# Banded attention, routing and two feed-forward layers on one core: gate products by two blocks, and idle matmuls in other places

## The chip, the cores and the metric

The program runs on one NeuronCore of a Trainium2 chip. TensorE (PE) multiplies; its weight loads are shown apart as PEld. VectorE (DVE), ScalarE (ACT) and GpSimd (POOL) work on vectors, and SyncE (SP) issues most DMAs. The metric is the device time of one launch in microseconds (us). Shorter is better.

## What is computed

Three stages follow each other: attention with a window of 128 and 4 sink keys, a mixture of 8 experts in which every expert takes exactly 192 of the 1536 tokens, and a dense layer with silu. The reference, cut:

```python
def _attn_ref(q, k, v, n_sink, window):          # q, k, v: (2, 8, 768, 64)
    ...
    keep = is_sink | in_window
    scores = np.where(keep, scores, -1000000000.0)
    ...
    return np.matmul(a, v).astype(np.float32)

def _moe_ref(x, w_gate, w1, w2):                 # x: (1536, 512), w_gate: (512, 8)
    logits = x @ w_gate
    order = np.argsort(-logits.flatten())        # best pair first, 192 tokens for each expert
    ...
        h = np.maximum(x[mask] @ w1[e], 0.0)
        out[mask] = h @ w2[e]

def _moe2_ref(x, w_in, w_out):                   # w_in: (512, 2048)
    h = x @ w_in
    g = h * (1.0 / (1.0 + np.exp(-h)))
    return (g @ w_out).astype(np.float32)
```

The gate's logits are linear in the attention's output. So the kernel multiplies the values with the gate's weights once (a "gate product": 8 extra columns for each head), and the attention's product with the values then yields the logits beside the output.

## The kernel before

**Attention** (`attention_band`) goes over 12 blocks of 128 queries (two batches of six) with 8 heads each. One loop over `n`, one step for each block and head, writes the order of all engines by hand: each engine works through its instructions in the order in which this loop issues them. In step `n` it issues the scores of heads `n` and `n+1` (`s_mm`, even `n`, L255), the exponential of head `n-2` on ACT (L277), the transposition of head `n-5` (`tr`, L291), then row maxima on DVE (L268), and at the end of the step the product of head `n-13` with the values (`pv`, L334 for the block's own keys, L336 for the block before, L339 for the sinks). Three queues (`act_now`, `act_bg`, `dve_now`) hold small pieces of work, of which `feed` takes one at a time between the large ones. Hooks at some `n` unpack weights of the last layer on DVE (L854 to L870).

The gate products stand in `vw`, once for each block `i`, eight steps after the block begins (`VL`): four matmuls (L374) with the transposed values as stationary operand (128 columns, a fresh one for each pair of heads) and 16 gate columns as moving operand, then one copy on ACT (L375) into columns `D:D+E` of `va`, which `pv` reads from step `8i + 13` on. `sinks` takes the first four rows of a batch's first block from there (L380 to L383).

PSUM is shared: the pool's name "s" has four buffers, for scores, for `misc()` (gate products, sinks, `sink_tr`) and for the routing.

**Routing** (`Route`) finds a threshold for each expert. Two shortened rounds run in the last steps of attention, then `run` makes four full rounds (`iterate`). A round is a chain: DVE chooses (L587 to L604), DVE and ACT compare with a grid (L622, L627), PE counts (L635), DVE decides (L644), PE raises the thresholds (L645). `result` then ranks the tokens (L751, L753), makes one-hot rows `R` on DVE (L777) and multiplies them on PE (L778, L781) into `idx`, by which POOL gathers the rows of the first experts (L965).

`warm(k)` issues `k` idle matmuls of 512 columns on PE (L796), whose result nobody reads. `HOLD` says how many stand behind each of the first three full rounds (10), behind the last one (4) and behind the gather (18); `HOT` how many stand between the ranks and the product with `R` (4). PE works strictly in this order, so what stands behind idle matmuls starts after them.

**Experts and dense layer**: `gathered_t` transposes gathered rows (L1002; two more idle matmuls after each of the first two, L1006), then long rows of matmuls follow (L1039, L1042 and others) until the end.

Of the kernel before, what the change touches and what calls it, by code (L numbers as in the profile page):

```python
# [11 lines left out]
F32 = mybir.dt.float32  # L12
# [3 lines left out]
AF = mybir.ActivationFunctionType  # L16
# [5 lines left out]
P = 128  # L22
B, H, S, D = 2, 8, 768, 64
NB = S // P
NT = B * NB
DM = H * D
KW = P + 4
E = 8
# [152 lines left out]

VW = D + E + 1
HH = H // 2
LT, LP, LS, VL = 5, 13, 6, 8
PB = {"s": 4, "tp": 2, "X": 2}
WARM = (8,) + (2,) * 5

# [1 line left out]
def attention_band(tc, qd, kd, va_d, vt_d, vs_d, sel_d, wbd_d, eye_d, n_sink, ident, x_d, L_sb, pp, hooks={}):  # L189
    nc = tc.nc  # L190
    with ExitStack() as ctx:
        cp = ctx.enter_context(tc.tile_pool(name="a_c", bufs=1))
        wp = ctx.enter_context(tc.tile_pool(name="a_w", bufs=2))

        kall = cp.tile([P, NB, HH, KW], F32, name="kall")
        va = cp.tile([P, NB, H, VW], F32, name="va")
        vts, Q = {}, {}

        def load(i, step=HH):
            b, j = divmod(i, NB)  # L200
            Q[i] = wp.tile([P, HH, P], F32, name="qr", bufs=4)
            for p in range(0, HH, step):
                nc.sync.dma_start(kall[:, j, p:p + step], kd[b, j][:, p:p + step])
                nc.sync.dma_start(Q[i][:, p:p + step], qd[b, j][:, p:p + step])

        def load_v(i):
            b, j = divmod(i, NB)
            vts[i] = wp.tile([P, 4, P], F32, name="vt", bufs=3)
            nc.sync.dma_start(vts[i], vt_d[b, j])
            nc.sync.dma_start(va[:, j], va_d[b, j])  # L210

        load(0, 1)
        wbd = cp.tile([P, 4, 2 * E], F32, name="wbd")
        nc.scalar.dma_start(wbd, wbd_d)
        sel = cp.tile([4, 96], F32, name="sel")
        nc.scalar.dma_start(sel, sel_d)
# [23 lines left out]
        nc.gpsimd.affine_select(out=mask[:, 1, 4:4 + n_sink], in_=mask[:, 1, 4:4 + n_sink], pattern=[[-1, n_sink]],  # L240
                                compare_op=OP.is_ge, fill=NEG, base=0, channel_multiplier=1)

        A, TS, AT, X, XS, LW = {}, {}, {}, {}, {}, {}
        ats = [cp.tile([97, P], F32R, name=f"ats{k}") for k in range(2)]
        for t in ats:
            nc.gpsimd.tensor_copy(t[96:97, :], later[0:1, 0:1].to_broadcast([1, P]))
# [1 line left out]
        def s_mm(n):  # L248
            i, h = divmod(n, H)
            j = i % NB  # L250
            b0 = max(j - 1, 0)
            for o in range(2):
                s = pp.tile([P, 512], F32, name="s", bufs=PB["s"])[:, :2 * KW].rearrange("p (a k) -> p a k", a=2)
                d = slice(o * D, (o + 1) * D)
                nc.tensor.matmul(s[:, :j - b0 + 1], Q[i][d, h // 2], kall[d, b0:j + 1, h // 2], start=True, stop=True)  # L255
                TS[n + o] = s
# [29 lines left out]
        def tr(n):  # L286
            i, h = divmod(n, H)
            g, r = divmod(h, 4)
            if r == 0:
                AT[i, g] = pp.tile([P, 4, P], F32, name="tp", bufs=PB["tp"])  # L290
            nc.tensor.transpose(AT[i, g][:, r], A[i][:, h, 4:], ident)  # L291
            if r == 3:
                act_now.append(lambda: tr_out(i, g))
# [9 lines left out]
                                        base=0, channel_multiplier=1)  # L303
            AT[i, g] = f, d

        def misc():
            return pp.tile([P, 512], F32, name="s", bufs=PB["s"])[:, :P]

        zero = cp.tile([P, 512], BF, name="zero")
        nc.vector.memset(zero, 0.0)  # L310
# [3 lines left out]
        def warm(k):  # L314
            for _ in range(k):
                nc.tensor.matmul(idle, zero[:, :P], zero, start=True, stop=True)
# [50 lines left out]
                dve_now.append(lambda: nc.vector.tensor_reduce(L_sb[:, i], lw.rearrange("p h e -> p e h"), AX.X,  # L367
                                                               OP.add))

        def vw(i):  # L370
            j = i % NB
            pf = misc()[:, :H * E]
            for c in range(4):
                nc.tensor.matmul(pf[:, c * 2 * E:(c + 1) * 2 * E], vts[i][:, c], wbd[:, c], start=True, stop=True)  # L374
            act_now.append(lambda: nc.scalar.activation(va[:, j, :, D:D + E], pf.rearrange("p (h e) -> p h e", h=H),  # L375
                                                        AF.Copy))

        def sinks(b):
            m = misc()[:96, :H * E].rearrange("p (h e) -> p h e", h=H)
            nc.tensor.matmul(m, sel, va[0:4, 0, :, D:D + E], start=True, stop=True)  # L380
            dve_now.append(lambda: nc.vector.tensor_tensor(vsf[b][:96, :, D:D + E], m, eye, OP.mult))
            dve_now.append(lambda: nc.vector.tensor_copy(vsr[b], vsf[b]))
            dve_now.append(lambda: nc.vector.tensor_tensor(vsr[b][64:96], vsf[b][64:96],  # L383
                                                           vsr[b][64:96].bitcast(F32), OP.subtract))

        def feed(*qs):
            for q in qs:
                if q:
                    f = q.popleft()
                    if f:  # L390
                        f()
                    return

        act_now, act_bg, dve_now = deque(), deque(), deque()
        warm(WARM[0])
        NH = NT * H
        for n in range(NH + LP + 5):
            i, h = divmod(n, H)
            if n < NH and n % 2 == 0:
                s_mm(n)  # L400
            if n < len(WARM) - 1:
                warm(WARM[n + 1])
            for f in hooks.get(n, ()):
                if f is None:
                    while dve_now:
                        feed(dve_now)
                else:
                    f()
            if 0 <= n - 2 < NH:
                s_exp(n - 2)  # L410
            if 0 <= n - LT < NH:
                tr(n - LT)
            feed(act_now, act_bg)
            if n < NH and n % 2 == 0:
                s_merge(n)
                s_merge(n + 1)
            feed(dve_now)
            if n < NH:
                s_max(n)
            feed(dve_now)  # L420
            feed(act_now, act_bg)
            it, ht = divmod(n - LS, H)
            if ht == H - 1 and 0 <= it < NT:
                sink_tr(it)
            if n < NH and h == 0:
                if i == 1:
                    nc.sync.dma_start(vsf[1][:96], vs_d[:96, 1])
                if i + 2 < NT:
                    load_v(i + 2)
                if i + 3 < NT:  # L430
                    load(i + 3)
            it, ht = divmod(n - VL, H)
            if ht == 0 and 0 < it < NT and it != NB:
                vw(it)
            if n in (VL + 2, NB * H + VL - 5):
                vw(n // (NB * H) * NB)
            if n in (VL + 4, NB * H + VL - 3):
                sinks(n // (NB * H))
            if 0 <= n - LP < NH:
                pv(n - LP)  # L440
        while act_now or act_bg or dve_now:
# [14 lines left out]
)  # L456
NA, RP = 4, 6
HOT, HOLD = 4, (10, 4, 18)


def levels(low, high):
# [24 lines left out]
class Route:  # L486
# [30 lines left out]
    def open(self, wp, psum):  # L517
        self.wp, self.psum = wp, psum
        self.it = 0
        self.work = None  # L520
        self.V = wp.tile([P, NT, E], F32, name="V", bufs=1)

    def scale(self, L, n):
# [122 lines left out]
        ]  # L646
        return steps, [partial(grid_act, t) for t in range(na)] + grids, counts, rise

    def iterate(self, na):
        for part in self.iteration(NT, na):  # L650
            for s in part:
                s()

# [7 lines left out]
    def run(self, L, idx, nit, more, bg=lambda k: None, speculate=lambda: None):  # L661
        self.work = self.psum("s")
        for k in range(nit):
            bg(k)
            self.iterate(NA)
            self.warm(HOLD[k + 1 == nit])
            if k == 0:
                self.scaled()
        bg(nit)
        badi = self.result(idx)  # L670
        speculate()
        self.warm(HOLD[2])
        self.further(badi, L, idx, more, speculate)

    def result(self, idx):
# [113 lines left out]
        nc.vector.scalar_tensor_tensor(idx.rearrange("p m s -> p s m"), im[:, :, 0], float(P), idf, OP.mult, OP.add)  # L789
        return badi  # L790

    def warm(self, k):
        m = self.psum("tp")
        g = self.G[:, :4].rearrange("p t h -> p (t h)")
        for _ in range(k):
            self.nc.tensor.matmul(m, self.onesb, g, start=True, stop=True)  # L796

# [496 lines left out]
def lay_out_band(x):  # L1294
    c = np.ascontiguousarray
    v, wg = x["v"], x["moe_w_gate"]
    va = np.zeros((B, NB, P, H, VW), v.dtype)
    va[..., :D] = v.transpose(0, 2, 1, 3).reshape(B, NB, P, H, D)
    va[..., D + E] = 1.0
    vs = np.zeros((97, B, H, VW), v.dtype)  # L1300
    vr = vs[:96].reshape(3, H, 4, B, H, VW)
    eye = np.zeros((3, H, 4, H, E), np.float32)
    for h in range(H):
        vr[:, h, :, :, h, :D] = v[:, h, :4].transpose(1, 0, 2)
        vr[:2, h, :, :, h, D + E] = 1.0
        eye[:, h, :, h, :] = 1.0
    vs[96, :, :, D + E] = 1.0e-9
    wbd = np.zeros((2, D, 4, 2, E), wg.dtype)
    for o in range(2):
        wbd[o, :, :, o, :] = wg.reshape(4, 2, D, E)[:, o].transpose(1, 0, 2)  # L1310
    return {
        "va": va,
        "vt": c(v.transpose(0, 1, 3, 2).reshape(B, 4, 2 * D, NB, P).transpose(0, 3, 2, 1, 4)),
        "vs": vs,
        "sel": np.tile(np.eye(4, dtype=np.float32), (1, 24)),
        "wbd": wbd.reshape(P, 4, 2 * E),
        "eye": eye.reshape(96, H, E),
    }

# [49 lines left out]
```

## Time and profile before

| | |
|---|---|
| time, three runs | 571.62, 571.73, 574.24 us (median 571.73) |
| the profiled execution | 575.38 us, of which its span is 573.7 us |
| PE busy | 558.0 us (97%) |
| DVE busy | 301.8 us (53%) |
| ACT busy | 259.5 us (45%) |
| POOL busy | 228.2 us (40%) |
| attention in that span | to 110.3 us |
| four full rounds, ranks, gather | 111.7 to 145.4 us |
| experts and dense layer | from 145.4 us on |

A time in the profile is a time from the start of the span. Busy shares are averages over stages with different limits; what binds a stage is read in it alone. The granted clock (PEclk) is a share of TensorE's full 2.4 GHz: 1.00 or 0.50 (1.2 GHz).

### The profile page before, as it was taken

To read this page: it belongs to the slowest core of one execution; us is meant where nothing else is said; L and a number is where in the kernel's file an instruction comes from. 1 tells how busy PE (TensorE), PEld (TensorE's weight loads), DVE (VectorE), ACT (ScalarE), POOL (GpSimd) and SP (SyncE) were. 2 spreads that over 40 slices of the span, in tenths; PEclk is the share of its full clock that TensorE was granted. 3 is DMA by queue.
4 is the path that set the end of the run, shared out by engine and by line. 5 is a ranking of instruction groups with operands and counts; after the bars stand their busy time and mean duration, and the time that the engine had idled before them with its cause. 6 is when DMAs were issued, how large, how long until landed. Compare 5 with 4: busy or idle time off the path is not lost.

```text
span 573.7 us, 9287 instructions
## 1 busy us (share of the span) xinstructions
PE 558.0 (97%) x3398; PEld 492.4 (86%) x3398; DVE 301.8 (53%) x855; ACT 259.5 (45%) x498; POOL 228.2 (40%) x207
## 2 busy tenths in 40 slices
PE   9999999789999999999999999999999999999996
PEld 4778778634899999999999998998899899899884
DVE  3796898973434443443338774665438843141312
ACT  4545454562467776776653452442222332222120
POOL 3434334394599999999993000000000000000224
PEclk9999999986999999999999999999999999999998
DMA  7997562244456666667661340323010000000012
GB/s 223 361 373 253 191 200 92 93 154 125 130 188 231 220 223 219 215 226 231 210 206 37 120 129 9 111 78 107 0 38 1 0 1 0 1 0 2 37 74 110
DMA packets 26367, 74.86 MB, mean 130 GB/s; under 512 B 3338, under 2 KB 4874, under 8 KB 26316
## 3 DMA queue, kind: packets, MB, share of 16 engines
q1 hardware_dynamic: 24128, 67.85, 35.8%
q0 software_dynamic: 1920, 6.29, 3.2%
q8 instruction: 29, 0.48, 0.4%
q14 instruction: 22, 0.18, 0.1%
q10 hardware_dynamic: 268, 0.06, 0.1%
HBM read 67.90 MB, written 6.29 MB: 129 GB/s over the span
## 4 chain that ended last, share of the span: by engine, by line
PE 68%; issue 3%; POOL 3%; ACT 1%; DVE 1%; POOLq 0%; another core or an unknown queue 0%; ACTq 0%
PE mm L1039 8%; PE m L1062 8%; PE h L1118 7%; PE h L1120 7%; PE h L1119 7%; PE acc L1148 7%; PE acc L1149 7%; PE acc L1147 7%; PE mm L1042 4%; PE m L1065 3%; POOL out L1131 2%; PE mm L1062 1%; PE mm L1002 1%; PE mm L1065 1%; POOL wr L895 0%
## 5 line engine op out<-in xcount | busy, mean ns | idle before, releaser
L895 POOL TENSOR_TENSOR wr<-raw,wr 128x1024 fp32r<-128x1024 f32 x64 | 150.9, 2389 | 10.7 <-ACT wr L892 7.1
L1131 POOL DMA_INDIRECT out<-osum,idx x12 | 11.8, 980 | 251.8 <-DVE osum L1155 250.7
L1122 ACT ACTIVATE sg<-h 128x384 f32<-128x384 f32 x64 | 31.4, 491 | 170.2 <-PE h L1120 156.4
L1124 DVE TENSOR_TENSOR gt<-sg,gt 128x384 fp32r<-128x384 f32 x64 | 39.3, 615 | 123.2 <-ACT gt L1123 122.7
L1118 PE MATMUL h<-x,wr 128*128 128x384 f32 x256 | 86.6, 338 | 0.0
L1119 PE MATMUL h<-x,wr 128*128 128x384 f32 x256 | 86.6, 338 | 0.0
L1120 PE MATMUL h<-x,wr 128*128 128x384 f32 x256 | 86.5, 338 | 0.0
L1039 PE MATMUL mm<-xg,wr 128*128 128x384 f32 x256 | 74.8, 362 | 1.6 <-DVE ht L1024 1.1
L1148 PE MATMUL acc<-wr,gt 128*128 128x512 f32 x192 | 76.0, 396 | 0.0
L1149 PE MATMUL acc<-wr,gt 128*128 128x512 f32 x192 | 76.0, 396 | 0.0
L1147 PE MATMUL acc<-wr,gt 128*128 128x512 f32 x192 | 76.0, 396 | 0.0
L892 ACT ACTIVATE wr<-raw 128x1024 fp32r<-128x1024 f32 x64 | 66.7, 1052 | 9.3 <-ACTq L681 6.8
L1062 PE MATMUL m<-ht,wr 128*128 128x384 f32 x224 | 66.1, 362 | 0.0
L1042 PE MATMUL mm<-xg,wr 128*128 128x192 f32 x256 | 64.3, 251 | 0.0
L1065 PE MATMUL m<-ht,wr 128*128 128x192 f32 x224 | 56.3, 252 | 0.0
L277 ACT ACTIVATE A<-t,nm 128x132 f32<-128x132 f32 x96 | 36.4, 400 | 33.7 <-DVE nm L268 33.4
L1039 PEld LDWEIGHTS mm<-xg,wr 128*128 128x128 f32 x256 | 48.1, 188 | 2.5 <-PE mm L1042 1.0
L1119 PEld LDWEIGHTS h<-x,wr 128*128 128x128 f32 x256 | 48.1, 188 | 1.4
L1118 PEld LDWEIGHTS h<-x,wr 128*128 128x128 f32 x256 | 48.1, 188 | 1.3
L1042 PEld LDWEIGHTS mm<-xg,wr 128*128 128x128 f32 x256 | 49.0, 191 | 0.1
L1120 PEld LDWEIGHTS h<-x,wr 128*128 128x128 f32 x256 | 48.1, 188 | 0.0
L1149 PEld LDWEIGHTS acc<-wr,gt 128*128 128x128 f32 x192 | 36.1, 188 | 8.7
(160 smaller groups left out, 1014.5 us busy)
## 6 DMA issues: line engine op xcount, KB each, us to landing
raw<-in_w SPq DMA_DIRECT2D x64, 512.0 KB, 3.6
raw<-in_wi SPq DMA_DIRECT2D x16, 512.0 KB, 3.9
raw<-in_wo SPq DMA_DIRECT2D x16, 512.0 KB, 4.2
va<-in_va SPq DMA_DIRECT2D x12, 292.0 KB, 5.0
vt<-in_vt SPq DMA_DIRECT2D x12, 256.0 KB, 4.7
x_d<-x SPq DMA_DIRECT2D x12, 256.0 KB, 3.2
kall<-in_kd SPq DMA_DIRECT2D x10, 264.0 KB, 5.4
qr<-in_qd SPq DMA_DIRECT2D x10, 256.0 KB, 5.6
```

The lines of the kernel that those rows point to most:

```text
L892: nc.scalar.activation(w[:, 0, sl], src(), AF.Copy)
L895: (nc.vector if k in self.late else nc.gpsimd).tensor_tensor(w[:, 1, sl], src(), w[:, 0, sl].bitcast(F32), OP.subtract)
L1039: nc.tensor.matmul(mm[:, b, :2 * CAP], w[:, 0, fb, d, o:o + P], x[:, d].rearrange("p a t -> p (a t)"), start=d == 0, stop=False, skip_grou ...
L1042: nc.tensor.matmul(mm[:, b, :CAP], w[:, 1, fb, d, o:o + P], x[:, d, 0], start=False, stop=d == 3, skip_group_check=True)
L1062: nc.tensor.matmul(mm[:, d % 2, :2 * CAP], w[:, 0, d // 2, f, o:o + P], ht[:, f].rearrange("p a t -> p (a t)"), start=c == 0 and f == 0, s ...
L1065: nc.tensor.matmul(mm[:, d % 2, :CAP], w[:, 1, d // 2, f, o:o + P], ht[:, f, 0], start=False, stop=last, skip_group_check=True)
L1118: nc.tensor.matmul(hv, w[:, 0, d, o:o + P], x2[:, d, 0, sx], start=d == 0, stop=False)
L1119: nc.tensor.matmul(hv, w[:, 0, d, o:o + P], x2[:, d, 1, sx], start=False, stop=False)
L1120: nc.tensor.matmul(hv, w[:, 1, d, o:o + P], x2[:, d, 0, sx], start=False, stop=d == 3)
L1147: nc.tensor.matmul(a, gt[:, 0, ts], w[:, 0, f], start=f == 0, stop=False)
L1148: nc.tensor.matmul(a, gt[:, 0, ts], w[:, 1, f], start=False, stop=False)
L1149: nc.tensor.matmul(a, gt[:, 1, ts], w[:, 0, f], start=False, stop=f == 3)
```

## The change

Gate products are made for two blocks at a time. The values of two blocks now stand side by side in one tile. The gate's weights are the stationary operand, padded with zeros to 32 columns for each pair of heads; the four pairs of heads write to partitions 0, 32, 64 and 96 of one PSUM tile, so each uses its own group of 32 columns of the PE array. The moving operand is the values, 256 columns. Since this gives the products transposed, ACT copies them to SBUF (`vwt`), two steps of the loop later PE transposes them back (`vw_tr`), and ACT writes one piece for each block to `va`. The table `VWS` says at which step each part stands: blocks 0 and 1 singly (8, 10, 13, 16), the pairs `m` = 1 to 5 at `16m + 5` and `16m + 8`; the sinks at 11 and 58 (12 and 53 before).

In the routing, 12 idle matmuls stand ahead of the first full round's counts, 5 behind each of the first three rounds (10 before), 6 behind the last one (4), 3 between ranks and product (4), and 26 behind the gather (18).

```diff
-LT, LP, LS, VL = 5, 13, 6, 8
+LT, LP, LS = 5, 13, 6
+VWS = {8: [((0, (0,)), 0)], 10: [((0, (0,)), 1)], 11: [((0,), 2)], 13: [((0, (1,)), 0)], 16: [((0, (1,)), 1)],
+       58: [((1,), 2)]}
+for m in range(1, NT // 2):
+    VWS[2 * H * m + 5], VWS[2 * H * m + 8] = [((m,), 0)], [((m,), 1)]
...
         def load_v(i):
             b, j = divmod(i, NB)
-            vts[i] = wp.tile([P, 4, P], F32, name="vt", bufs=3)
-            nc.sync.dma_start(vts[i], vt_d[b, j])
+            if i % 2 == 0:
+                vts[i // 2] = wp.tile([P, 4, 2, P], F32, name="vt", bufs=2)
+            nc.sync.dma_start(vts[i // 2][:, :, i % 2], vt_d[b, j])
             nc.sync.dma_start(va[:, j], va_d[b, j])
...
-        def vw(i):
-            j = i % NB
-            pf = misc()[:, :H * E]
+        def vw(m, os=(0, 1)):
+            k = len(os)
+            pf = misc(k * P)
             for c in range(4):
-                nc.tensor.matmul(pf[:, c * 2 * E:(c + 1) * 2 * E], vts[i][:, c], wbd[:, c], start=True, stop=True)
-            act_now.append(lambda: nc.scalar.activation(va[:, j, :, D:D + E], pf.rearrange("p (h e) -> p h e", h=H),
-                                                        AF.Copy))
+                nc.tensor.matmul(pf[c * 4 * E:(c + 1) * 4 * E], wbd[:, c],
+                                 vts[m][:, c, os[0]:os[-1] + 1].rearrange("p o t -> p (o t)"),
+                                 start=True, stop=True, skip_group_check=True)
+            f = VT[m, os] = wp.tile([P, 2 * P], F32, name="vwt", bufs=1)
+            act_now.append(lambda: nc.scalar.activation(f[:, :k * P], pf, AF.Copy))
+
+        def vw_tr(m, os=(0, 1)):
+            k = len(os)
+            pt = misc(k * P).rearrange("p (o z) -> p o z", o=k)
+            f = VT.pop((m, os))
+            for q in range(k):
+                nc.tensor.transpose(pt[:, q], f[:, q * P:(q + 1) * P], ident)
+
+            def put(q, o):
+                nc.scalar.activation(
+                    va[:, (2 * m + o) % NB, :, D:D + E].rearrange("p (c k) e -> p c k e", k=2),
+                    pt[:, q].rearrange("p (c k e) -> p c k e", c=4, e=E)[:, :, :2], AF.Copy)
+            act_now.extend(partial(put, q, o) for q, o in enumerate(os))
...
-            it, ht = divmod(n - VL, H)
-            if ht == 0 and 0 < it < NT and it != NB:
-                vw(it)
-            if n in (VL + 2, NB * H + VL - 5):
-                vw(n // (NB * H) * NB)
-            if n in (VL + 4, NB * H + VL - 3):
-                sinks(n // (NB * H))
+            for at, f in VWS.get(n, ()):
+                (vw, vw_tr, sinks)[f](*at)
...
-HOT, HOLD = 4, (10, 4, 18)
+HOT, HOLD = 3, (12, 5, 6, 26)
...
-    def iterate(self, na):
-        for part in self.iteration(NT, na):
+    def iterate(self, na, warm=0):
+        g = self.G
+        parts = self.iteration(NT, na)
+        self.warm(warm if g is not None else 0, g)
+        for part in parts:
...
-            self.iterate(NA)
-            self.warm(HOLD[k + 1 == nit])
+            self.iterate(NA, HOLD[0] if k == 0 else 0)
+            self.warm(HOLD[1 + (k + 1 == nit)])
...
-        self.warm(HOLD[2])
+        self.warm(HOLD[3])
```

The first place is PE at a block in the middle of attention, eight steps after an even block began (X is the product with the values, tp a transposition, s the shared PSUM name). Before:

```order
L255 MATMUL s<-kall,qr 128x264 x2
L291 MATMUL tp<-ident,A 128x128
L374 MATMUL s<-wbd,vt 128x16 x4
L334 MATMUL X<-va,atd 128x73
L336 MATMUL X<-va,at 128x73
L339 MATMUL X<-vsr_144,ats_158 128x292
```

In the changed kernel the same stretch of PE, from step `16m + 5` to `16m + 8`:

```order
L325 MATMUL s<-ident,a_1183 96x128
L379 MATMUL s<-vt,wbd 32x256 x4
L339 MATMUL X<-va,atd 128x73
L341 MATMUL X<-va,at 128x73
L260 MATMUL s<-kall,qr 128x264 x2
L296 MATMUL tp<-ident,A 128x128
L339 MATMUL X<-va,atd 128x73
L341 MATMUL X<-va,at 128x73
```

The four matmuls of 16 columns, once a block, became four of 256 columns and 32 rows of output, once in two blocks. They stand right behind the sinks' transposition, and one product with the values (L339, L341) parts them from the next scores (L260). Two transpositions follow three steps later, where L374 stood.

The second place is ACT over the same steps (A the exponentials, at the evacuated transposition). Before:

```order
L277 ACTIVATE A<-t,nm 128x132 x4
L297 ACTIVATE at<-tp 128x512
L277 ACTIVATE A<-t,nm 128x132
L375 ACTIVATE va<-s 128x8x8
L277 ACTIVATE A<-t,nm 128x132 x3
```

In the changed kernel:

```order
L302 ACTIVATE at<-tp 128x512
L282 ACTIVATE A<-t,nm 128x132 x2
L383 ACTIVATE vwt<-s 128x256
L282 ACTIVATE A<-t,nm 128x132 x2
L302 ACTIVATE at<-tp 128x512
L282 ACTIVATE A<-t,nm 128x132
L393 ACTIVATE va<-s 128x8x8 x2
```

Two copies for two blocks became one of 256 columns and two small ones; the large one stands behind two exponentials and an evacuation.

The third place is PE where the first full round begins (G the grid, r_dlt the thresholds' steps). Before, the counts follow the last raising at once:

```order
L635 LDWEIGHTS G
L635 MATMUL s<-oh,G 128x8
L645 LDWEIGHTS r_dlt
L645 MATMUL s<-sel,r_dlt 128x8
L635 LDWEIGHTS G
L635 MATMUL s<-oh,G 128x8
```

In the changed kernel the idle matmuls stand between, of which one is shown and 12 are issued; the counts (L650) follow them:

```order
L650 LDWEIGHTS G
L650 MATMUL s<-oh,G 128x8
L660 LDWEIGHTS r_dlt
L660 MATMUL s<-sel,r_dlt 128x8
L816 LDWEIGHTS r_ones
L816 MATMUL tp<-G,r_ones 128x512
```

The counts of the first full round moved behind 12 matmuls that wait for nothing.

## Rows read from the trace of the kernel before

**Rows 1.** Windows by stage: length, then busy us of each engine, clock, DMA.

```profile
core 0: us, PE busy (x) PEld busy (x) DVE busy (x) ACT busy (x) POOL busy (x), PEclk, DMA share, GB/s
20.00:52.00 32.00, 32.00 (x253) 25.93 (x251) 26.34 (x137) 15.19 (x42) 12.68 (x27) 1.00 0.90 326
60.00:76.00 16.00, 16.00 (x112) 12.22 (x110) 15.69 (x73) 8.21 (x21) 5.98 (x12) 1.00 0.56 189
100.00:110.00 10.00, 10.00 (x98) 9.51 (x97) 9.59 (x50) 5.19 (x14) 4.59 (x9) 1.00 0.33 107
112.95:119.75 6.80, 4.68 (x23) 2.01 (x24) 5.36 (x16) 4.97 (x11) 3.74 (x2) 0.50 0.13 49
130.00:140.20 10.20, 9.95 (x64) 5.48 (x65) 3.90 (x23) 3.49 (x4) 2.37 (x3) 0.50 0.30 87
```

**Rows 2.** Timeline of PE: start, us, tile sizes, count; scores of 264 columns.

```profile
99.77 0.39 PE L336 MATMUL X<-va,at 128*128 128x73 f32 x2
100.90 0.34 PE L334 MATMUL X<-va,atd 128*128 128x73 f32 x2
101.08 0.39 PE L336 MATMUL X<-va,at 128*128 128x73 f32 x2
101.41 0.34 PE L334 MATMUL X<-va,atd 128*128 128x73 f32 x2
```

**Rows 3.** Timeline of PE around scores of 132 columns.

```profile
57.56 0.39 PE L336 MATMUL X<-va,at 128*128 128x73 f32 x2
58.47 0.34 PE L334 MATMUL X<-va,atd 128*128 128x73 f32 x2
```

**Rows 4.** Timeline of PE's weight loads around one block's gate products.

```profile
101.84 1.00 PEld L374 LDWEIGHTS s<-wbd,vt 128*128 128x128 f32 x8
102.76 0.30 PEld L334 LDWEIGHTS X<-va,atd 128*128 128x128 f32 x2
```

**Rows 5.** Instructions of L781, two 64-column groups each time: ns min/median/max.

```profile
L781 PE MATMUL X<-ohp,R x24: 213/215/216, 132.7 to 135.7; 128*64 128x8 bf16 x24
```

**Rows 6.** ACT by form, 8 to 112 us: count, busy us, mean ns, idle before.

```profile
L297 ACT ACTIVATE at<-tp 128x512 f32<-128x512 f32 x24 | 14.3, 596 | 17.7 <-PE tp L291 17.6
L375 ACT ACTIVATE va<-s 128x64 f32<-128x64 f32 x12 | 2.7, 223 | 1.1 <-PE s L374 1.1
```

**Rows 7.** Timeline of PE, start of the full rounds.

```profile
114.72 0.86 PE L635 MATMUL s<-oh,G 128*128 128x8 bf16 x12 [2.90 <-DVE G L622]
115.87 4.23 PE L796 MATMUL tp<-G,r_ones 128*128 128x512 bf16 x10
120.63 0.17 PE L645 MATMUL s<-sel,r_dlt 128*128 128x8 bf16 x1 [0.26 <-DVE sel L644]
120.66 2.32 PE L796 MATMUL tp<-G,r_ones 128*128 128x512 bf16 x10
124.74 0.17 PE L645 MATMUL s<-sel,r_dlt 128*128 128x8 bf16 x1 [0.26 <-DVE sel L644]
```

**Rows 8.** Timeline of PE and DVE, last round to first expert.

```profile
128.84 0.17 PE L645 MATMUL s<-sel,r_dlt 128*128 128x8 bf16 x1 [0.26 <-DVE sel L644]
130.25 0.26 PE L751 MATMUL tp<-oh,r_tri 128*128 128x96 bf16 x1 [0.36 <-DVE oh L598]
131.56 2.24 DVE L777 TENSOR_SCALAR R<-r_slot,r 128x192 bf16<-128x192 bf16 x12
132.56 0.22 PE L778 MATMUL X<-ohp,R 128*128 128x16 bf16 x1
135.87 6.20 PE L796 MATMUL tp<-G,r_ones 128*128 128x512 bf16 x18
142.95 0.63 PE L1002 MATMUL mm<-ident,row 128*128 128x128 f32 x4 [0.88 <-PEq L681]
```

**Rows 9.** POOL's gather of the experts' rows: ns min/median/max, and issue to landing.

```profile
L965 POOL DMA_INDIRECT row<-x_d,idx x4: 942/956/1177, 137.2 to 145.8; - x4
...
DMA to landing us min/median/max: 3.5/4.5/5.1
```

More of the change, by code (lines that the diff above doesn't have):

```diff
@@ L207, in load_v @@
             b, j = divmod(i, NB)
-            vts[i] = wp.tile([P, 4, P], F32, name="vt", bufs=3)
-            nc.sync.dma_start(vts[i], vt_d[b, j])
+            if i % 2 == 0:
+                vts[i // 2] = wp.tile([P, 4, 2, P], F32, name="vt", bufs=2)
+            nc.sync.dma_start(vts[i // 2][:, :, i % 2], vt_d[b, j])
             nc.sync.dma_start(va[:, j], va_d[b, j])
         load(0, 1)
-        wbd = cp.tile([P, 4, 2 * E], F32, name="wbd")
+        wbd = cp.tile([P, 4, 4 * E], F32, name="wbd")
         nc.scalar.dma_start(wbd, wbd_d)
@@ L241, in attention_band @@
                                 compare_op=OP.is_ge, fill=NEG, base=0, channel_multiplier=1)
-        A, TS, AT, X, XS, LW = {}, {}, {}, {}, {}, {}
+        A, TS, AT, X, XS, LW, VT = {}, {}, {}, {}, {}, {}, {}
         ats = [cp.tile([97, P], F32R, name=f"ats{k}") for k in range(2)]
@@ L304, in tr_out, with misc @@
             AT[i, g] = f, d
-        def misc():
-            return pp.tile([P, 512], F32, name="s", bufs=PB["s"])[:, :P]
+        def misc(k=P):
+            return pp.tile([P, 512], F32, name="s", bufs=PB["s"])[:, :k]
         zero = cp.tile([P, 512], BF, name="zero")
@@ L519, in open @@
         self.it = 0
-        self.work = None
+        self.work = self.G = None
         self.V = wp.tile([P, NT, E], F32, name="V", bufs=1)
@@ L790, in finish, with warm @@
         return badi
-    def warm(self, k):
+    def warm(self, k, g=None):
+        if not k:
+            return
         m = self.psum("tp")
-        g = self.G[:, :4].rearrange("p t h -> p (t h)")
+        g = (self.G if g is None else g)[:, :4].rearrange("p t h -> p (t h)")
         for _ in range(k):
@@ L1307, in lay_out_band @@
     vs[96, :, :, D + E] = 1.0e-9
-    wbd = np.zeros((2, D, 4, 2, E), wg.dtype)
+    wbd = np.zeros((2, D, 4, 4, E), wg.dtype)
     for o in range(2):
@@ L1315, in lay_out_band @@
         "sel": np.tile(np.eye(4, dtype=np.float32), (1, 24)),
-        "wbd": wbd.reshape(P, 4, 2 * E),
+        "wbd": wbd.reshape(P, 4, 4 * E),
         "eye": eye.reshape(96, H, E),
```

## The prediction

> **What bounds the kernel now.** I read the windows by stage first, since the shares over the whole span mix three different stages. In attention PE is busy 32.00 us of 32.00, 16.00 of 16.00 and 10.00 of 10.00, at the full clock [rows 1]: what PE saves there is the first candidate for a gain. But DVE (the third column, behind PE's weight loads) has 26.34 of 32, then 15.69 of 16 and 9.59 of 10 [rows 1]. From 60 to 76 us PE could shorten its work and gain 0.31 us at most before DVE sets the pace, and in the last 10 us 0.41. Behind attention nothing is busy throughout: the rounds are a chain, and there I read the timeline of PE for what stands in front of the chain's next matmul [rows 7, 8]. PE's clock is 0.50 in 112.95 to 119.75 and again in 130.00 to 140.20 [rows 1], so an idle matmul costs 2.32/10 = 0.23 us where the clock is full and 4.23/10 = 0.42 where it is half [rows 7]. The experts behind the gather start when L1002 does, at 142.95 [rows 8], and from there on the change touches nothing.
>
> **Gate products.** One block costs PE 102.76 - 101.84 = 0.92 us [rows 4], so two cost 1.84. The new form appears in no row; I build it from three. (1) Columns: with scores of 264 columns, L336 to L334 takes 100.90 - 99.77 = 1.13 us, without scores 101.41 - 101.08 = 0.33 [rows 2], so scores cost 0.80; with 132 columns 58.47 - 57.56 - 0.33 = 0.58 [rows 3]. The difference, 0.22 us for 132 columns in two passes, is 0.83 ns for a column and pass; 256 columns in two passes are 0.43 us. (2) What is left of the scores, 0.80 - 0.44 = 0.36, is the price of going to another tile size and back. (3) A transposition of 128 columns, two passes of a fresh matmul, is about 0.92/8 = 0.11 us [rows 4].
> If the four column groups run side by side, a pair costs 0.36 + 0.43 + 2 x 0.11 = 1.01 and saves 0.83; a single block costs 0.36 + 0.21 + 0.11 = 0.68 and saves 0.24. If they run one after the other, a pair costs 0.36 + 4 x 0.43 + 0.22 = 2.30 and loses 0.46, a single 1.32 and loses 0.40. L781 is the nearest row: two matmuls on two 64-column groups take 0.215 us each [rows 5], and twelve times one L778 with two of them take 135.87 - 132.56 = 3.31 us [rows 8], 0.28 for three matmuls and the change of tile there and back, at the half clock. Three in a row would not fit, so groups do overlap, and the change of tile may cost less than 0.36. But there only 8 columns stream. I take side by side and 0.36.
>
> The Trainium skill (TensorE: Matmul & The Clock Gate, Part 3, Packing small matmuls) gives 2.38 times for three column tiles instead of 3. By it, as an estimate, the 0.43 would be 0.54, and five pairs would save 0.5 us less. Its page TensorEngine Tiling (Array Packing), Tiling Modes, says that going to another tiling mode drains TensorE, which speaks against this change; the 0.36 of the scores agrees and is in the sum.
>
> **Where these savings land.** Five pairs and two singles could save 5 x 0.83 + 2 x 0.24 = 4.6 us. Pairs 1 and 2 lie before 60 us, where PE sets the pace: 1.66 us. Attention's 108 steps end at 110.3 us, at about 1 us a step, so pairs 3 to 5 (steps 53, 69 and 85) and what they replace (to step 96) stand from about 57 us on; with DVE's 0.31 and 0.41 of room in its two tight windows I choose 0.9 for the three, a third of their 2.5. Against it: at the start, blocks 0 and 1 and the sinks now pass PE, ACT, PE, ACT instead of PE, ACT; one more ACT copy (between 0.22 and 0.60 [rows 6]) and its way there and back, about 0.3 us lost. And a wait is new: the gate products take a buffer of "s", and the scores one step later need it free, so they wait for ACT's copy, which stands behind two exponentials and an evacuation (0.60 [rows 6]), with the rest of one step between (a step without scores takes 101.41 - 100.90 = 0.51 [rows 2]). Queued behind the scores on PE are the next transposition and product, so a late copy stops all of PE. I take 0.4 us over the pairs; below 0 and above 5 x 0.3 = 1.5 I see nothing. Attention: -1.66 - 0.9 + 0.3 + 0.4 = **-1.9 us**. Bounds: -4.6 if all lands and nothing waits; +3.8 if the groups run one by one (5 x 0.46 + 2 x 0.40 + 0.7). The values arrive in smaller pieces, but their issue stands some 16 steps, about 16 us, ahead of their use; I count nothing, and without that cover only the first block's would show.
>
> **Routing, step by step.** (a) Twelve idle matmuls ahead of the first counts: PE sat 2.90 us for G there [rows 7]. At the full clock 12 x 0.23 = 2.8 us fit: 0; at the half clock 5.1 us would add 2.2. The clock fell at 112.95 only after a stretch in which PE had little to do, and now PE is busy from the stretch's start: I take 0. (b) Behind the first round, ten at the half clock took 4.23 us and held the counts back: that round lasted 120.63 - 115.87 = 4.76 us, the next 124.74 - 120.63 = 4.11 [rows 7]. Five fit at either clock (1.2 or 2.1): **-0.65**. Fewer idle matmuls in the other rounds gain nothing, since the chain through DVE sets the 4.11. (c) Behind the last round, six instead of four: the ranks start 130.25 - 128.84 = 1.41 us after L645 [rows 8]. At the full clock six take 1.4, nothing; at the half clock 2.5: **+1.1**. (d) Three instead of four between ranks and product: 0.42 less at the half clock, where PE and not R came last (R's first piece was there a little after 131.56, PE came at 132.56 [rows 8]): **-0.42**. (e) The product, 3.31 us at the half clock, would take some 1.0 to 1.8 us less at the full one, where DVE's 2.24 us for R bound it [rows 8]. (f) Behind the gather 26 instead of 18: L1002 came right behind the 18 and the queue's 0.88 (135.87 + 6.20 + 0.88 = 142.95 [rows 8]). The rows landed 3.5 to 5.1 us after POOL's issue at 137.2 and later [rows 9], so they were hardly later than PE. Eight more at the full clock, to which it had risen after 140.2, are 8 x 0.23 = **+1.8**.
> Which clock holds? With ten idle a round PE kept the full clock from 119.75 to 130.0, and it fell in the stretch with only four [rows 1, 7]. Now each round has five. I expect the half clock from the second or third round through the product, so (b), (c), (d) and (f) count as marked: -0.65 + 1.1 - 0.42 + 1.8 = **+1.8 us**.
>
> **Sum.** -1.9 + 1.8 = -0.1 us. The profiled execution took 575.38 us, 3.65 above the median of the three runs, 571.73; the profile so gives the difference and the median the level: **571.6 us**. Half a per cent, 2.9 us, is about what a measurement of this kernel can tell from no change.
>
> **Rivals.**
> A, the forecast (0.45): overlap in attention, given back by six and 26 idle matmuls at a late clock: 571.6, by itself 570 to 573.2.
> B, faster (0.27): twelve ahead and five a round are enough to hold the full clock. Then (c) costs nothing, (e) gives 1.4, and 26 at 0.23 take 6.0 us, less than the 6.20 of before: -0.65 - 1.4 - 0.2 = -2.2, with attention -4.1: about 567.7. For it: the clock fell only where PE had long gaps. Against it: it fell, too, in the stretch with four.
> C, slower (0.10): the column groups run one by one. +3.8 + 1.8: 577.3. It decides from the point where four matmuls of 256 columns take over about 1.3 us together. Against it: L781's overlap.
> D, slower (0.09): the first twelve run at the half clock and hold the counts, +2.2 on A: 573.8.
> E, no gain in attention (0.09): DVE paces it, or the scores' new wait takes 1.5 and more: +1.8, 573.5.
> B makes up faster (with a piece of A's lower end, less B's nearer half); C and parts of D and E make up slower: 0.25, 0.59 and 0.16. The range leaves out C and the outer halves of B and D: 567.4 to 574.4.
>
> **What would show it.** Right: the four new matmuls of a pair start within 0.1 us of each other, and the next product with the values starts 0.8 us after; blocks before 60 us take some 0.4 us less than before on average, and from 60 to 76 us the same; scores behind a pair wait up to 0.3 us for the copy; all rounds take 4.1; the ranks come 2.6 us behind the last L645; L1002 starts right behind the 26. Wrong: the four start 0.4 us apart (C); PE's clock 1.00 from the first round to the product (B); the first counts later than 2.9 us behind L645 (D); an attention that ends later than 109.5 us (E). An effect on the experts' stage, which I hold unchanged, would upset the sum as well.

## The result and the profile after

The changed kernel takes 577.28 us (median of 6 runs, 576.93 to 578.32); the kernel before took 572.66 (6 runs, 571.62 to 575.68). The ratio is 1.0077, interval 1.0049 to 1.0106: 4.4 us slower. In the sets of runs further down, a few executions take 591 us or more at a lower clock; the medians include them, the ratios leave them out. The profiled execution took 577.28 us, its span 575.6, which is 1.9 us more than the profiled span of before; that profile was of one of the longer runs of the kernel before (575.38 us), and the experiments show below what its runs differ by.

The first view is PE's timeline of the changed kernel, at one pair's gate products in the middle of attention, and near the end of attention the sinks' transposition (L325) without them (start, us, operation):

```profile
54.04 0.27 PE L325 MATMUL s<-ident,a 128*96 128x128 f32 x1
54.24 0.64 PE L379 MATMUL s<-vt,wbd 128*32 128x256 f32 x8
54.81 0.44 PE L339 MATMUL X<-va,atd 128*128 128x73 f32 x2
...
57.81 0.38 PE L390 MATMUL s<-ident,vwt 128*128 128x128 f32 x2
58.03 0.34 PE L339 MATMUL X<-va,atd 128*128 128x73 f32 x2
...
96.40 0.27 PE L325 MATMUL s<-ident,a 128*96 128x128 f32 x1
96.51 0.34 PE L339 MATMUL X<-va,atd 128*128 128x73 f32 x2
```

With a pair, L325 to L339 takes 54.81 - 54.04 = 0.77 us, without 0.11: the pair's matmuls cost 0.66 us of PE, and the two transpositions 58.03 - 57.81 = 0.22. That is 0.88 against 1.84 for two blocks before [rows 4]. Eight passes of 256 columns in 0.57 us from the first to the next product cannot have run one after another, at 0.21 us each: the four column groups overlap.

The second view is windows of 2 us at the end of attention: in the kernel before and then in the changed one (length, busy us of PE, PEld, DVE, ACT and POOL, granted clock, DMA share, GB/s).

```profile
102.00:104.00 2.00, 2.00 (x20) 2.00 (x20) 1.83 (x10) 1.17 (x4) 1.03 (x2) 1.00 0.87 287
106.00:108.00 2.00, 2.00 (x27) 1.92 (x26) 1.90 (x11) 1.75 (x3) 1.53 (x2) 1.00 0.07 28
```

```profile
100.00:102.00 2.00, 2.00 (x21) 1.92 (x20) 1.90 (x8) 0.65 (x2) 1.62 (x5) 1.00 0.50 189
102.00:104.00 2.00, 0.82 (x13) 0.64 (x11) 2.00 (x4) 1.76 (x3) 1.66 (x2) 1.00 0.01 4
104.00:106.00 2.00, 1.88 (x14) 1.85 (x14) 1.90 (x13) 0.00 (x0) 0.00 (x0) 0.73 0.27 103
106.00:108.00 2.00, 2.00 (x11) 2.00 (x11) 1.42 (x11) 0.56 (x3) 0.00 (x0) 0.50 0.08 28
```

In the changed kernel PE is busy for 0.82 of 2.00 us from 102 to 104, the counts of the first shortened round, while DVE is busy for all of it. The kernel before comes to the same counts only at 106.20 us, and there PE is busy throughout. In the changed kernel the clock is at half from 104.9 us on, 8 us earlier than in the profile of before [rows 1]. The counts, and the last raising ahead of the full rounds, in the profile of before:

```profile
106.20 0.49 PE L635 MATMUL s<-oh,G 128*128 128x8 bf16 x10
...
111.65 0.17 PE L645 MATMUL s<-sel,r_dlt 128*128 128x8 bf16 x1 [0.26 <-DVE sel L644]
```

The third view is PE's timeline of the changed kernel from there to the first expert; the bracket is PE's idle time and who ended it.

```profile
102.32 0.25 PE L650 MATMUL s<-oh,G 128*128 128x8 bf16 x4
103.35 0.26 PE L650 MATMUL s<-oh,G 128*128 128x8 bf16 x4 [0.78 <-DVE G L637]
104.12 0.21 PE L650 MATMUL s<-oh,G 128*128 128x8 bf16 x2 [0.52 <-DVE G L637]
...
109.60 0.63 PE L341 MATMUL X<-va,at 128*128 128x73 f32 x2
...
111.14 0.17 PE L660 MATMUL s<-sel,r_dlt 128*128 128x8 bf16 x1 [0.27 <-DVE sel L659]
111.16 4.72 PE L816 MATMUL tp<-G,r_ones 128*128 128x512 bf16 x12
115.72 0.45 PE L650 MATMUL s<-oh,G 128*128 128x8 bf16 x12
116.42 0.17 PE L660 MATMUL s<-sel,r_dlt 128*128 128x8 bf16 x1 [0.26 <-DVE sel L659]
...
120.60 0.17 PE L660 MATMUL s<-sel,r_dlt 128*128 128x8 bf16 x1 [0.26 <-DVE sel L659]
...
128.83 0.17 PE L660 MATMUL s<-sel,r_dlt 128*128 128x8 bf16 x1 [0.25 <-DVE sel L659]
128.85 2.72 PE L816 MATMUL tp<-G,r_ones 128*128 128x512 bf16 x6
131.37 0.29 PE L769 MATMUL tp<-oh,r_tri 128*128 128x96 bf16 x1
...
135.98 7.30 PE L816 MATMUL tp<-G,r_ones 128*128 128x512 bf16 x26
145.04 0.63 PE L1022 MATMUL mm<-ident,row 128*128 128x128 f32 x4 [1.76 <-PEq L699]
```

PE waits for DVE's grid G for 0.78 and 0.52 us in the first shortened round; after that a product with the values (L341) takes 0.63 us instead of 0.39 [rows 2], and the 12 idle matmuls take 4.72 us. The first full round, 111.14 to 116.42, takes 5.28 us. The second is 4.18 against 4.76 [rows 7], the ranks stand 131.37 - 128.83 = 2.54 us behind L660 against 1.41 [rows 8], and L1022 comes 2.09 us later than before [rows 8].

### The profile page after: what moved, and what is told of

Its sections match the earlier page's. It is cut to its first block, busy times and chain, and to the rows that moved or that the text cites. A ratio compares the mean times of both kernels' runs of the same rounds, so it can differ in the third digit from the quotient of the medians.

```text
span 575.6 us, 9262 instructions
## 1 busy us (share of the span) xinstructions
PE 557.7 (97%) x3376; PEld 487.5 (85%) x3376; DVE 301.5 (52%) x855; ACT 260.9 (45%) x505; POOL 228.7 (40%) x207
## 4 chain that ended last, share of the span: by engine, by line
PE 67%; issue 3%; POOL 3%; ACT 1%; DVE 1%; POOLq 0%; another core or an unknown queue 0%; ACTq 0%
PE mm L1059 8%; PE m L1082 8%; PE h L1138 7%; PE h L1140 7%; PE h L1139 7%; PE acc L1168 7%; PE acc L1169 7%; PE acc L1167 7%; PE mm L1062 4%; PE m L1085 3%; POOL out L1151 2%; PE mm L1082 1%; POOL wr L915 1%; PE mm L1022 1%; PE mm L1085 1%
```

## The experiments

The theory after the result: with the new gate products PE runs ahead of DVE, so it waits in attention's last steps, the clock falls there, and the rest of attention and the 12 idle matmuls run at half speed; the 26 cost what they last. The rival: the new idle matmuls alone are the loss. Ratios are to the kernel before, run beside each set on the same chip; its median was 573.99 us beside the first four kernels below, 573.80 beside the next four and 573.53 beside the last four.

**The parts alone.**

```diff
 # gate products only: the changed kernel with
-HOT, HOLD = 3, (12, 5, 6, 26)
+HOT, HOLD = 4, (0, 10, 4, 18)
 # idle matmuls only: the kernel before with iterate, run and warm of the changed kernel, and
-HOT, HOLD = 4, (10, 4, 18)
+HOT, HOLD = 3, (12, 5, 6, 26)
```

> The changed kernel's gate products with the idle matmuls of before (none ahead of the first full round, 10, 4 and 18, four between ranks and product). Theory: in the changed kernel PE runs about 4 us ahead of DVE by 101 us, so in attention's last steps it waits for the grid of the first shortened round (0.78 and 0.52 us), the clock falls to 0.50 at about 105 us, the rest of attention runs at half speed, and what was won is given back there. By it this kernel falls to 0.50 before 108 us as well, its last raising before the full rounds (L660) ends within 1 us of the 111.65 of before, and the whole takes 571 to 576 us, no clear gain over before. Rival: the gate products are a plain gain of 3 to 4 us and the idle matmuls alone cost what the change loses; then the clock holds past 111 us, L660 is at about 108, and the time is about 569.

Measured: 573.76 us, ratio 1.0003 (0.9982 to 1.0024). PE waited the same 0.78 and 0.52 us, the clock fell at 104.1 us, and the last L660 ahead of the full rounds stood at 111.06. The theory holds: the gate products alone win nothing that can be measured, since what they win is lost in the same place.

> The gate products of before with the changed idle matmuls (12, 5, 6, 26 and three). Theory: attention is as before, its clock holds to the end, so 12 idle matmuls ahead of the first counts run at the full clock (0.22 us each) and hide; 26 behind the gather cost 8 x 0.22 = 1.7 us more, six behind the last round up to 1.1 if the clock is at half there; the second round is shorter by 0.65. Time: 0 to 2.5 us above before, 573 to 575. Rival: these numbers are the whole loss, and it is 4 us or more above before, 577, with the 12 at the half clock (5 us) here too.

Measured: 576.52 us, ratio 1.0054 (1.0036 to 1.0072): about 3 us, more than the theory gave and less than the rival. No profile of it is read here. The two parts together give 1.0077, 1.1 us more than the sum of the two. The first full round of the changed kernel lasted 5.28 us with the 12 at half clock, and 111.06 to 115.31, 4.25, with the gate products alone: 1.0 us, which would be that remainder; but the intervals are wide enough for a remainder of nothing.

**The gaps filled.** Six idle matmuls where PE waited for G:

```diff
         w = len(steps) // 3
+        if not na:
+            g = route.G
+            counts = [counts[0], lambda: route.warm(4, g), counts[1], lambda: route.warm(2, g), counts[2]]
```

> The changed kernel, with four idle matmuls behind the first piece and two behind the second piece of the counts of the first shortened round (where PE waited 0.78 and 0.52 us for the grid, at 102.5 to 104.1 us). Theory: the gaps there let the clock fall; filled, it stays at 1.00 to the end of attention, which then ends about 2 us earlier, the 12 idle matmuls take 2.7 instead of 4.72 us, and the experts start 3 us or more earlier: 571 to 574.5 us, 3 to 6 less than the changed kernel. Rival: the fall is owed to the 73-column products of the last steps as such, whatever stands in the gaps: it comes at the same place, and the time stays at 577 or goes up by up to 1 us.

Measured: 575.43 us, ratio 1.0025 (1.0005 to 1.0044), 3.0 us less than the changed kernel's 1.0077. PE's timeline of this kernel:

```profile
102.68 1.02 PE L816 MATMUL tp<-G,r_ones 128*128 128x512 bf16 x4
...
103.72 0.59 PE L816 MATMUL tp<-G,r_ones 128*128 128x512 bf16 x2
...
109.53 0.17 PE L660 MATMUL s<-sel,r_dlt 128*128 128x8 bf16 x1 [0.26 <-DVE sel L659]
109.56 4.44 PE L816 MATMUL tp<-G,r_ones 128*128 128x512 bf16 x12
```

The interval lies below that of the changed kernel. The clock now fell at 109.89 us and L660 stands at 109.53 instead of 111.14. The theory is right on the gaps and the tail, and wrong on the 12: the fall came just as they began, and they still took 4.44 us.

**The kernel before once more.**

> The kernel before once more, unchanged, for a second profile: its runs stand at 571.6 to 571.8 and at 573.6 to 575.7 us. Theory: these differ by where the clock falls and rises between 110 and 140 us; a profile at about 571.7 has the clock at full in more of 112.9 to 140.2 than the profile of 575.38, and experts that start about 3.5 us before 145.45. Rival: they differ behind 145 us, at the end or in DMA, and the clock's course is the same.

Measured: 571.65 us. This execution is the kernel of [rows 7, 8] again, with another course of the clock (fall at 111.2, rise at 118.1, and no further fall before the end):

```profile
110.85 0.17 PE L645 MATMUL s<-sel,r_dlt 128*128 128x8 bf16 x1 [0.26 <-DVE sel L644]
...
133.31 4.06 PE L796 MATMUL tp<-G,r_ones 128*128 128x512 bf16 x18
138.48 0.63 PE L1002 MATMUL mm<-ident,row 128*128 128x128 f32 x4 [1.10 <-DMA row<-x_d,idx]
...
141.99 0.45 PE L1039 MATMUL mm<-xg,wr 128*128 128x384 f32 x1 [0.47 <-DVE xg L1013]
```

The 18 take 4.06 instead of 6.20 us, and L1002, now waiting for the rows, comes 4.5 us earlier than in [rows 8]. The first product of the experts (L1039) comes 3.5 us earlier than the 145.45 of the other profile. Of this 0.8 us was there before the clock fell in either (L645 at 110.85 against 111.65), and from the first gate product on (L374 at 11.56 against 12.35); the other 2.7 us arise between there and 142 us, where the course of the clock differs.

**Single numbers of the routing.**

```diff
-HOT, HOLD = 3, (12, 5, 6, 26)
+HOT, HOLD = 3, (12, 5, 6, 18)   # 18 behind the gather
+HOT, HOLD = 3, (0, 5, 6, 26)    # none ahead of the first full round
```

> The changed kernel with 18 instead of 26 idle matmuls behind the gather, all else as changed. In its profile the 26 end at 143.28 us and the first expert's L1022 stands at 145.04, while the rows were issued at 137.33 and land 3.5 to 4.7 us later. Theory: the 26 and what follows them on PE's queue hold the experts back; eight fewer give 8 x 0.22 = 1.7 us, up to 2.6 if the 1.76 us behind them fall to the 0.9 of before: the ratio to before goes from 1.008 to about 1.004, 1.7 to 2.6 us less. Rival: the rows or the weights bound the experts' start there, and it stays at 1.008.

Measured: 574.88 us, ratio 1.0027 (1.0005 to 1.0049), 2.9 us less than the changed kernel, though the two intervals touch. The wait on PE's queue behind the 18 was 0.88 us. From the first of the 18 to L1022 its profile has 144.15 - 136.73 = 7.42 us, where the changed kernel has 145.04 - 135.98 = 9.06: 1.64 us less. The 26 do hold the experts back.

> The changed kernel without the 12 idle matmuls ahead of the first full round, all else as changed. Theory: since the clock is at half there, the 12 take 4.72 us where 2.9 to 3 us were idle, and cost 1.1 us net; without them the first round is 4.2 us instead of 5.28, and with nothing else in the first round the clock rises no earlier, so the gain is 1 us or less: ratio 1.006 to 1.008. Rival: the 12 lift the clock for the rounds and the product behind them; without them the time rises by 0.5 us or more.

Measured: 575.41 us, ratio 1.0038 (1.0012 to 1.0063), 2.2 us less. The sign is the theory's and the size above it; the interval is too wide to say by how much. In its profile the first full round is 110.19 to 114.44, 4.25 us.

**Towards a better version.** The filled gaps with the old numbers, and then with the clock held into the rounds as well:

```diff
 # filled gaps as above, and
+HOT, HOLD = 4, (0, 10, 4, 18)
 # filled gaps, two ahead of the second shortened round's counts, and
+        else:
+            counts = [lambda: route.warm(2, VG[0])] + counts
+        VG.append(route.G)
+HOT, HOLD = 4, (12, 10, 4, 18)
```

> The changed gate products, the six idle matmuls in the gaps of attention's last steps (four and two behind pieces of the first shortened round's counts), and the routing's idle matmuls as before (none, 10, 4, 18, and four). Theory: the gate products' gain of 2.3 us is kept when the clock holds through attention, and the rounds go as in the kernel before: 2 to 3 us below before, ratio 0.995 to 0.997. Rival: the lead is lost again in a later fall of the clock, as the second shortened round waits for DVE anyway: ratio 1.000 as with the gate products alone.

Measured: 572.16 us, ratio 0.9985 (0.9967 to 1.0002): less of a gain than expected, and its interval reaches 1. The clock held to 112.2 us, past attention.

> As the kernel with the idle matmuls in the tail and the old numbers, and two more idle matmuls ahead of the second shortened round's counts and 12 ahead of the first full round's. Theory: where the clock is still full at 109.5 us the 12 take 2.7 us, hide, and keep it full through the first rounds; the second round is then 4.1 instead of 4.8 us, and the experts start where the rows let them: ratio 0.992 to 0.996. Rival: the clock has fallen by then, as in the profile with the tail filled (109.89 us), the 12 take 4.4 us and cost 1.1 us: ratio 0.998 or above, worse than without them.

Measured: 571.18 us, ratio 0.9967 (0.9948 to 0.9986). The clock stayed full from 6 us to 132.5 us. The 12 took 2.75 us here, and the rounds 4.1 to 4.2.

The last four ran side by side on one chip.

```diff
 # the version before this, with the changed kernel's numbers
+HOT, HOLD = 3, (12, 5, 6, 26)
 # the kernel before (old gate products), two ahead of the second shortened round's counts, and
+HOT, HOLD = 4, (12, 10, 4, 18)
```

> The new gate products with the filled tail, two ahead of the second shortened round's counts, 12 ahead of the first full round's and the old numbers behind (10, 4, 18 and four), on the same chip as the other three. Theory: 0.995 to 0.998, with the interval below 1, and 2 us below the kernel with the old gate products and the 12. Rival: the first comparison was luck of the clock's course, and it stands at 1.000.

Measured: 570.73 us, ratio 0.9956 (0.9936 to 0.9976). It stands below 1 a second time, on another chip, so the first comparison was not luck.

> The kernel before, its gate products kept, with two idle matmuls ahead of the second shortened round's counts and 12 ahead of the first full round's (the others as before: 10, 4, 18 and four). Theory: the new gate products are worth 2 us where the clock is held in both kernels; so this one, which holds it too, is about 2 us above the kernel with the new gate products and the filled tail, at ratio 0.999 to 1.001. Rival: what the filled-tail kernel won is owed to the 12 and the clock alone; then this one stands at 0.995 to 0.997 as well.

Measured: 573.48 us, ratio 1.0000 (0.9979 to 1.0020). With the clock held through the rounds in both, the new gate products are worth 0.44%, 2.5 us; the 12 and the two alone are worth nothing measurable. PE's timeline of the two kernels at the first shortened round's counts, where the full rounds begin, and behind the gather, first this one, then the one with the new gate products:

```profile
105.50 0.50 PE L635 MATMUL s<-oh,G 128*128 128x8 bf16 x10
...
110.96 0.17 PE L645 MATMUL s<-sel,r_dlt 128*128 128x8 bf16 x1 [0.26 <-DVE sel L644]
110.98 2.75 PE L801 MATMUL tp<-G,r_ones 128*128 128x512 bf16 x12
...
133.38 6.72 PE L801 MATMUL tp<-G,r_ones 128*128 128x512 bf16 x18
140.98 0.63 PE L1007 MATMUL mm<-ident,row 128*128 128x128 f32 x4 [0.88 <-PEq L684]
```

```profile
102.06 0.25 PE L650 MATMUL s<-oh,G 128*128 128x8 bf16 x4
...
109.02 0.17 PE L660 MATMUL s<-sel,r_dlt 128*128 128x8 bf16 x1 [0.26 <-DVE sel L659]
109.05 2.75 PE L816 MATMUL tp<-G,r_ones 128*128 128x512 bf16 x12
...
131.29 5.75 PE L816 MATMUL tp<-G,r_ones 128*128 128x512 bf16 x18
137.92 0.63 PE L1022 MATMUL mm<-ident,row 128*128 128x128 f32 x4 [0.88 <-PEq L699]
```

With the new gate products PE comes to the first counts 3.44 us earlier (102.06 against 105.50), is held there by DVE's grid, with idle matmuls filling the time, and ends attention 1.94 us earlier, all filling included. Some 0.1 us of it is an earlier start (the third group of scores stands at 7.83 against 7.95 us); the rest, 1.8 us, is the gate products'. The rounds then go alike. Behind them the clock is at half from 131.98 to 138.81 us in the first and from 131.65 to 135.06 in the second, and the 18 take 6.72 against 5.75 us; so the rows' first transposition comes 3.06 us earlier. Whether the new gate products have a part in this later difference is not shown.

> The changed kernel, its own numbers (12, 5, 6, 26 and three) kept, with six idle matmuls in the gaps of the first shortened round and two ahead of the second one's counts, so that the clock is full when the 12 begin. Theory: the 12 now hide (2.75 us), but five a round let the clock fall before the ranks, six then cost 1.1 us, and 26 with the longer wait behind them cost 2.5 to 3 us against 18: ratio 1.001 to 1.005. Rival: once the clock is full at the start, five a round hold it, 26 take 5.7 us, and the ratio is 0.997 as with the old numbers.

Measured: 574.65 us, ratio 1.0028 (1.0010 to 1.0046). The clock, full when the 12 began, fell at 116.4 us, in the rounds with five: the rival's condition is met and its result is not. The six then held the ranks back here too (129.03 - 126.49 = 2.54 us). The old numbers in its place are worth 0.72%, 4.1 us. PE's timeline of this kernel:

```profile
126.49 0.17 PE L660 MATMUL s<-sel,r_dlt 128*128 128x8 bf16 x1 [0.26 <-DVE sel L659]
...
129.03 0.29 PE L769 MATMUL tp<-oh,r_tri 128*128 128x96 bf16 x1
...
133.63 7.39 PE L816 MATMUL tp<-G,r_ones 128*128 128x512 bf16 x26
142.94 0.63 PE L1022 MATMUL mm<-ident,row 128*128 128x128 f32 x4 [1.91 <-PEq L699]
```

Beside the profile with the old numbers above, the ranks come 1.1 us later behind L660 (2.54 against 1.41), from the ranks to the idle matmuls behind the gather it is 4.60 against 4.30, and from these to L1022 9.31 against 6.63 us. Of these last 2.7 us, 1.6 are the idle matmuls and 1.0 the queue's wait behind them (1.91 against 0.88). In this pair of profiles the three make 4.1 us.

> The changed kernel once more, to stand beside the others on one chip. Both theories: 1.005 to 1.010; the clock falls between 103 and 107 us, and the first expert starts at 146.5 to 148 us.

Measured: 578.09 us, ratio 1.0076 (1.0054 to 1.0097), as at first. But the profiled run goes against the expectation: the clock fell at 117.1 us and the first expert's product stands at 143.87. This run, 573.84 us, is the odd one of its seven (the others 576.73 to 578.54). Its windows and its timeline:

```profile
102.00:104.00 2.00, 0.70 (x14) 0.52 (x13) 1.97 (x4) 1.52 (x3) 1.38 (x2) 1.00 0.01 4
106.00:108.00 2.00, 1.96 (x20) 1.69 (x19) 1.93 (x9) 1.50 (x7) 0.00 (x0) 1.00 0.00 0
```

```profile
101.98 0.24 PE L650 MATMUL s<-oh,G 128*128 128x8 bf16 x4
103.01 0.25 PE L650 MATMUL s<-oh,G 128*128 128x8 bf16 x4 [0.78 <-DVE G L637]
...
108.95 0.17 PE L660 MATMUL s<-sel,r_dlt 128*128 128x8 bf16 x1 [0.26 <-DVE sel L659]
108.97 2.75 PE L816 MATMUL tp<-G,r_ones 128*128 128x512 bf16 x12
...
133.00 7.47 PE L816 MATMUL tp<-G,r_ones 128*128 128x512 bf16 x26
141.41 0.63 PE L1022 MATMUL mm<-ident,row 128*128 128x128 f32 x4 [0.93 <-PEq L699]
```

The same program, with the same waits of 0.78 and 0.52 us, and here the clock held until 117.1: L660 is 2.2 us earlier than in the first profile, the 12 hide (the first full round takes 4.18 instead of 5.28 us), and the whole is 3.4 us shorter. It is the theory's counter-case, made by the chip, in one execution: without the early fall the loss is mostly gone, but the 26 and the rest still keep it from a gain.

## Why the prediction was wrong

The sum was -0.1 us, and the change made the kernel 4.4 us slower, beyond the range. Two steps of the prediction failed: (a), which put the fall of the clock at nothing, and the step to the level, "the profile so gives the difference and the median the level". By its own steps:

**Gate products, right.** The column groups overlap, a pair costs 0.88 us (1.01 was forecast). Case C falls. But the row from which the overlap was read did not show it: three matmuls of 0.215 us "would not fit" into 0.28 only if the times of single matmuls add up, and they do not on one tile size either (twelve of L635 take 0.86 us, one L645 of as many columns 0.17 [rows 7]). The conclusion was right by luck. By the Trainium skill (TensorE: Matmul & The Clock Gate, Part 3, Packing small matmuls) three column tiles gain 2.38 times; here four groups need at most 0.66 us, all changes of tile included, where one after another they would need 4 x 0.43 = 1.72 by the row's price, 2.6 times or more. The two do not contradict each other.

**Where the savings land, right in size, wrong in what follows.** Where the clock holds in both, attention ends 1.8 to 1.94 us earlier, against the -1.9 of the forecast. The agreement is in part luck: PE was 3.44 us ahead at the first shortened round's counts, more than forecast, and lost 1.5 of it there, waiting for DVE. The scores' wait for the new copy is 0.2 us in all, not 0.4. And I took DVE's tight windows only as a cap on the gain. That PE, where it is ahead of DVE, must wait somewhere, and where, I did not ask: it waits in the counts of the first shortened round, and PE's clock then falls within 3 us of the gap in four of the five profiles with the gap open; in the five with it filled it does not fall before 109.89 us.

**(a) is the first step that failed**: "now PE is busy from the stretch's start: I take 0". I started the question of the clock behind attention, and the fall comes inside it. From 104.9 us the tail runs at half speed, which costs about 1.9 us (from the first counts at 102.32 to L660 8.82 us, against 6.97 in the execution in which the clock held), and the 12 then take 4.72 us and cost 1.1. That is case D's mechanism for the 12, at half its price, with a tail at half speed before it that no case had. The gate products' gain is gone by it (ratio 1.0003 alone).

**(b) and (c), right**: the second round 4.18 us (about 4.1 expected), the ranks 2.54 us behind L660 (2.5 expected). **(d), too small**: the forecast had the half clock through the product, and the clock rose at 132.25 us, ahead of it. From the ranks to the idle matmuls behind the gather it is 135.98 - 131.37 = 4.61 us against 5.62 [rows 8]: 1.0 us less, where 0.42 was in the sum.

**(f), near enough.** From the first idle matmul behind the gather to L1022 it is 9.06 us against 7.08 [rows 8]: 1.98 us more, where 1.8 was in the sum; with the clock held it is 2.7. What (f) left out is that the queue's 0.88 us behind the idle matmuls can grow. The forecast put the idle numbers at +1.8 in all, and they cost 3.1 alone and 4.1 with the clock held.

**The level, the other step that failed.** Of the 4.6 us between the two medians (577.28 and 572.66), 1.9 stand between the two profiled executions, of which that of the changed kernel is at its median, and 2.7 between the profile of before (575.38) and its median. My sum took the differences from that profile, with the product at half clock and the 18 at 6.20 us, and added them to a median of shorter runs. Another execution of the same kernel keeps the clock full from 118 us on and starts the experts 3.5 us earlier, 2.7 of it by the clock. With five a round that course is gone (the fall at 116.4 us with everything else held). So the change also removed the better courses, a loss that a difference to one profile cannot contain. How the 3.1 us of the idle numbers alone split is not settled, since no profile of that kernel is read.

**B** is refuted in its condition: five a round do not hold the clock, even when it is full before them. In none of the six profiles read with five a round was it full to the end of the rounds; in all seven with ten it was, from the third round on at the latest.

## What to carry to other kernels

Work taken off PE makes PE early, and on this chip an early PE that waits is a PE whose clock may fall: ask at which instruction it will wait, and fill that gap, before counting the gain. Here the same gate products are worth nothing with the gap open (ratio 1.0003), about 1 us with six idle matmuls in it, which the interval does not part from nothing (0.9985), and 2.5 us, of which 1.8 are seen in attention, where further idle matmuls hold the clock through the rounds in both kernels. A term that hangs on the clock must not be taken from one profile: two executions of the same kernel differed by 2.7 us in it.

## What the hardware showed beside that

The same gap does not always bring the clock down: in one profile of the changed kernel it fell at 104.9 us, in another, with the same waits of 0.78 and 0.52 us, not before 117.1. Why is not shown. The Trainium skill (TensorE: Matmul & The Clock Gate, Part 1, What's actually happening) says that the monitor that sets PE's clock by its activity looks at a window that runs on its own and does not start with the kernel; the two profiles agree with that, and no run here shows the window itself.

Behind 18 idle matmuls PE's queue needs 0.88 to 0.93 us until the rows' first transposition, wherever the rows are not late (seven profiles, with the new gate products or the old). Behind 26 it took 1.76 us in the changed kernel, 2.24 with the gaps filled, 1.65 without the 12, 1.91 with the clock held and 0.93 in the last profile of the changed kernel. What the queue waits for there was not found; it is up to 1.3 us of the cost of the 26.
